# One form of softmax sums for all 24 head pairs, weight buffers released earlier, and two kinds of stores issued by GpSimd

## The chip, the cores and the metric

The kernel runs on one core of a Trainium2 chip (trn2). The metric is the device time in microseconds. A core has TensorE (PE, with its weight loads listed apart as PEld), VectorE (DVE), ScalarE (ACT), GpSimd (POOL) and SyncE (SP), which here issues nearly all transfers of the 16 DMA engines. Each engine takes its instructions in the order in which the program wrote them for it.

## The reference

Three layers run one after the other on 4 sequences of 448 tokens (12 heads of 64, 768 channels):

```python
scores = cap * tanh(q @ k.T / sqrt(64) / cap)
attn = exp(scores - scores.max(-1)); attn /= attn.sum(-1) + 1e-9
x = attn @ v                                   # per head, then 768 channels
...
xk = mu_k*x + (1-mu_k)*x_prev; xr = mu_r*x + (1-mu_r)*x_prev
v = relu(xk @ w_k)**2 @ w_v                    # 768 -> 1024 -> 768
x = sigmoid(xr @ w_r) * v
...
theta = x @ w_theta
y = w_tok_r @ (x*cos(theta)) + w_tok_i @ (x*sin(theta))
u = x + y
out = u + relu(u @ w_ch)
```

The weights come as 64-bit floats, and the kernel turns them into pairs of 16-bit halves (high and low) itself.

## The kernel before, in words

The whole program is a list of operations with engine, planned duration, rank, and the buffers read and written. `Plan.order` (L149) simulates it once on the host with the planned durations and takes, whenever an engine is free, the ready operation of lowest rank; the order that comes out is the program's order on every engine. All transfers stand in the plan as one queue named `DMA`; which engine issues one is decided by the call inside the operation (`nc.sync` is SP, `nc.gpsimd` would be GpSimd). Planned durations therefore move the order of everything, while real waits are semaphores.

**Attention (to about 365 us).** 24 pairs of heads, one after the other, with the products of the first layer of earlier sequences (`kmm`, `rmm`, in `units`, L783 to L785, three matmuls per step: high by high, high by low, low by high) filled in between. Of a pair, `scores` makes the scores (L649, L653), ACT takes tanh and exp, `attend` adds three of the four blocks on DVE (L739), and then one of two forms makes the sums over keys and their reciprocals. `narrow`, for the first 12 pairs (`WIDE = 12`): 16 small matmuls (L676, L680) put the sums of 8 groups of 112 queries on 8 bands of 16 rows, DVE takes a reciprocal of 112 columns (L687), and four matmuls with a 128-column weight (`spread`, L692) spread it over the rows; ACT or DVE brings the product with v out of PSUM (`avo`), and DVE multiplies (L704). `wide`, for the last 12: the fourth block is added first (`fold`, L745, two operations a pair), two matmuls of 448 columns (L712) give the sums on all rows, the reciprocal has 448 columns (L718), and one DVE operation scales the product (L729). Both take the product with v in 10 matmuls. Then come `mxd`, `mxk`, `mxh`, `mxl` (L751 to L758), which mix neighbouring tokens and split into halves.

**Second layer's values (about 417 to 560 us).** `values` (L893): `kd` is loaded again (L900) and split (`k2h`, `k2l`), `vmm` multiplies by w_v (24 matmuls for each of 24 units, two PSUM buffers), a stored gate is loaded into one of five buffers `z` (L906), ACT takes a sigmoid (L907), DVE multiplies (L909), and the store `stx` (L912) writes the result to DRAM. It is loaded again by L941 and L950. The buffer `z` is free when that store has landed.

**Third layer (about 468 us to the end).** `angles`, `mixes`, `channels`: matmuls at L957 to L959, L987 to L989, L1009 to L1011. At the end of a unit DVE adds (L1014), and `sto` (L1015) stores the result.

**Weights.** `group` (L515) and `tokens` (L863) load raw 64-bit weights into one of two buffers `w` (L530, L869), rebuild 32-bit values in one of three buffers `f` (`bits`: a rescaling, L454 to L458, then DVE L461, L464, L467), and take their size: `squares` (L491) squares them on ACT (L495) with an accumulated sum; the squares themselves are of no use, and are written over the raw buffer `w`. PE adds the sums (L500), and three small DVE operations follow. Then come high and low halves (`whi`, `wlo` L543, L885), which go into memory that opens late for w_theta and the token weights (`o_r2`, after the last pair) and for w_ch (`o_l2`, after the last `kmm` and `rmm`). The w_k weights take their size another way (`early`).

Of the kernel before, what the change touches and what calls it, by code (L numbers as in the profile page):

```python
# [7 lines left out]
F32 = mybir.dt.float32  # L8
# [4 lines left out]
AF = mybir.ActivationFunctionType  # L13
ALU = mybir.AluOpType
# [4 lines left out]
B, H, S, D = 4, 12, 448, 64  # L19
# [5 lines left out]
SH = S // 2  # L25
# [5 lines left out]
KT = 7  # L31
# [217 lines left out]
def v1(n):  # L249
    return 0.17 + n / 940.0  # L250
# [6 lines left out]
def act(n):  # L257
    return 0.17 + n / 1150.0
# [19 lines left out]
def body(nc, tc, exact, qk, v, cap, mu_k, mu_r, w_k, w_v, w_r, w_th, w_tr, w_ti, w_ch, out):  # L278
    P = Plan()
    op = P.op  # L280
    ENG = {"ACT": nc.scalar, "DVE": nc.vector, "POOL": nc.gpsimd}
    SLOT = 7.9
    WIDE = 12
    WV0, WV1 = 190.0, 28.0
    WT0, WT1, WO0, WC0, WC1 = 1440.0, 10.0, 1510.0, 1660.0, 20.0
    K20, VM0, VM1 = 390.0, 1500.0, 100.0
# [21 lines left out]
    def tt(n, half=False):  # L308
        return {"POOL": pool(n) - 0.00021 * n * half, "DVE": v1(n)}
# [4 lines left out]
    xd = [[Buf(tile=dr.tile([128, S], F32, name=f"xd{b}_{m}")) for m in range(KD)] for b in range(B)]  # L314
# [55 lines left out]
    def small(n=1):  # L370
        used[0] += n
        return Buf(tile=scal[:, used[0] - n:used[0]])
# [115 lines left out]
        op("PE", 0.3, rank, lambda: nc.tensor.matmul(ps.t[:, 0:1], unit[0:w].to_broadcast([w, 128]), d.t[0:w], start=True, stop=True), r=[d], w=[ps], name="bcast")  # L488
        return ps

    def squares(rank, parts, d):  # L491

        ps = Buf(c_ps)
        for a, (f, val, n, dead) in enumerate(parts):
            op("ACT", act(n) + 0.19, rank, lambda a=a, val=val, n=n, dead=dead: nc.scalar.activation(out=dead.t[:, 0:n], in_=val(), func=AF.Square, accum_out=d.t[:, a:a + 1]),  # L495
               r=[f] if f is not dead else [], w=[dead, (d, a)], name="norm")

        def total():
            for a in range(len(parts)):
                nc.tensor.matmul(ps.t[:, 0:1], unit.to_broadcast([128, 128]), d.t[:, a:a + 1], start=(a == 0), stop=(a == len(parts) - 1))  # L500
        op("PE", 0.2 + 0.1 * len(parts), rank, total, r=[d], w=[ps], name="bcast")
        return ps
# [12 lines left out]
    def group(rank, src, dst, m, inv, nb, after=(), early=False):  # L515

        sw, n = small(), 128 * nb
        vals, parts = [], []
        for a in range(len(dst)):
            w, f = Buf(w_s), Buf(f_s)  # L520
            vals.append(f)

            def half(i, w=w):
                return w.t[:, 0:2 * n].bitcast(U32).rearrange("p (n two) -> p n two", two=2)[:, :, i]

            def val(f=f):
                return f.t[:, 0:n]

            def ld(w=w, a=a):
                nc.sync.dma_start(out=w.t[:, 0:2 * n].bitcast(U32).rearrange("p (i n) -> p i n", i=nb),  # L530
                                  in_=src[n * a:n * a + n, 256 * m:256 * m + 256].rearrange("(i p) n -> p i n", p=128))
            op("DMA", 0.03 + n / 350, rank - 12, ld, w=[w], after=[o_open1], name="wld")
            bits(rank, lambda h=half: h(1), lambda h=half: h(0), val, val, n, w, f, f)
            parts.append((f, val, n, 128 if early else w))
        size(rank, grams(rank, [parts], small()) if early else squares(rank, parts, small(len(parts))), inv, m, sw)
        for a, f in enumerate(vals):
            def part(i, a=a):
                return dst[a].t[:, :, i, 128 * m:128 * m + 128]

            def val(f=f):  # L540
                return f.t[:, 0:n].rearrange("p (i n) -> p i n", i=nb)
            op({**cs(n), "DVE": (v1 if nb % 2 else v2)(n) + 0.06}, 0, rank, lambda e, val=val, part=part: copy(e, part(0), val(), sw.t), r=[f, sw], w=[(dst[a], (m, 0))], after=after, name="whi")
            grouped.append(op("DVE", v1(n) + 0.06, rank, lambda val=val, part=part: nc.vector.scalar_tensor_tensor(  # L543
                out=part(1), in0=val(), scalar=sw.t, in1=part(0), op0=ALU.mult, op1=ALU.subtract),
               r=[f, sw, (dst[a], (m, 0))], w=[(dst[a], (m, 1))], name="wlo"))
# [14 lines left out]
    for b in range(B):  # L560
        R = (2 * NP * b - 7.1) * SLOT if b else 3
        vb = v[NP * b:NP * b + NP].rearrange("g p n -> (g p n)").rearrange("(p n) -> p n", p=128)
        parts = []
        n = 2 * DM
        for c in range(2):
            t = Buf(w_s)
            op("DMA", 0.03 + n / 700, R - 10, lambda t=t, c=c, vb=vb: nc.sync.dma_start(out=t.t, in_=vb[:, c * n:(c + 1) * n]), w=[t], after=[o_open1], name="ldm")
            parts.append([(t, lambda t=t: t.t, n, 128)] if b == 0 else (t, lambda t=t: t.t, n, t))
        size(R, squares(R, parts, small(2)) if b else grams(R, parts, small()), small(), 0, sv[b])
        times(R, sv[b], qi, sx[b])  # L570
        inverse(R, sx[b], ix[b], 0.0, 2.0)
# [14 lines left out]
    last1 = []  # L586
# [79 lines left out]
            op("ACT", act(n * S) + 0.08, A + 3 + 1.8 * c, lambda th=th: nc.scalar.activation(out=th.t, in_=th.t, func=AF.Exp, scale=cap_t),  # L666
               w=[th], name="exp", table="exp")

    def narrow(A, x, sxb, th, vn, z, sp, rs, ps):

        def sums():

# [4 lines left out]
            for k in range(2):  # L677
                for h, i in ((0, 0), (0, 1), (1, 0), (1, 1)):
                    c = 32 * (2 * h + i)
                    nc.tensor.matmul(sp.t[c:c + 32, 0:SQ], ones[:, 1 + i, k], th[3].t[:, h, SQ * k:SQ * k + SQ], start=False, stop=(k == 1))  # L680
        op("PE", 0.74, A, sums, r=[z, th[3]], w=[sp], name="sums")

        def den():

# [5 lines left out]
        def spread():  # L690
            for i in range(4):
                nc.tensor.matmul(sp.t[:, SQ * i:SQ * i + SQ], live["row"][:, i].rearrange("p h d -> p (h d)"), rs.t, start=True, stop=True)  # L692
        op("PE", 0.8, A + 2, spread, r=[rs], w=[sp], name="spread")

        def av():
            for c in range(3):
# [6 lines left out]
        op({"ACT": act(S) + 0.09, "DVE": 0.7}, 0, A + 3, lambda e: copy(e, x.t[:, 1:S + 1], ps.t[:, 0:S], sxb.t), r=[ps, sxb], w=[x], name="avo")  # L703
        last1.append(op("DVE", v1(S), A + 6, lambda: nc.vector.tensor_tensor(out=x.t[:, 1:S + 1], in0=x.t[:, 1:S + 1], in1=sp.t[:, 0:S], op=ALU.mult), r=[sp], w=[x], name="norm"))  # L704

    def wide(A, x, sxb, th, vn, z, sp, ps):

        rs = lambda: x.t[:, 1:S + 1]

        def sums():  # L710
            for h in range(2):
                nc.tensor.matmul(sp.t[64 * h:64 * h + 64, 0:S], unit.to_broadcast([128, D]), z.t[:, h], start=True, stop=True, skip_group_check=True)  # L712
        op("PE", 0.74, A, sums, r=[z], w=[sp], name="sums")

        def den():
            if exact:
                nc.vector.tensor_scalar(out=rs(), in0=sp.t[:, 0:S], scalar1=1e-9, scalar2=None, op0=ALU.add)
            nc.vector.reciprocal(out=rs(), in_=rs() if exact else sp.t[:, 0:S])  # L718
        op("DVE", 2.95, A + 1, den, r=[sp], w=[x], name="den")

        def av():
            for c in range(3):
                for h in range(2):
                    nc.tensor.matmul(ps.t[64 * h:64 * h + 64, 0:S], vn.t[0][:, h, c], th[c].t[:, h], start=(c == 0), stop=False, skip_group_check=True)  # L724
            for i in range(2):
                for h in range(2):
                    nc.tensor.matmul(ps.t[64 * h:64 * h + 64, SH * i:SH * i + SH], vn.t[1][:, i, h], th[3].t[:, h], start=False, stop=True, skip_group_check=True)
        op("PE", 3.02, A + 0.5, av, r=[vn, *th], w=[ps], name="av")
        last1.append(op("DVE", v1(S) + 0.06, A + 4, lambda: nc.vector.scalar_tensor_tensor(  # L729
            out=x.t[:, 1:S + 1], in0=ps.t[:, 0:S], scalar=sxb.t, in1=rs(), op0=ALU.mult, op1=ALU.mult), r=[ps, sxb], w=[x], name="norm"))  # L730

    def attend(g):
        A = g * PAIR + 10
        th, vn = thb[g], vnb[g]
# [4 lines left out]
            op("DVE", v1(2 * S), A - 4 + i, lambda i=i: nc.vector.tensor_tensor(out=z.t, in0=th[0].t if i == 1 else z.t, in1=th[i].t, op=ALU.add),  # L739
               r=[th[0], th[1]] if i == 1 else [th[i]], w=[z], name="sum")  # L740

        if g >= WIDE:
            for i in range(2):
                p, q = slice(64 * i, 64 * i + 64), slice(SH * i, SH * i + SH)
                op(tt(S), 0, A - 1 + 0.5 * i, lambda e, p=p, q=q: e.tensor_tensor(out=z.t[p, :, q], in0=z.t[p, :, q], in1=th[3].t[p], op=ALU.add), r=[th[3]], w=[(z, i)], name="fold")  # L745
            wide(A, x, sx[b], th, vn, z, sp, ps)
        else:
            narrow(A, x, sx[b], th, vn, z, sp, rs, ps)
        R = A + 7
        d, t0 = Buf(mx_s), Buf(mx_s)  # L750
        op(tt(S), 0, R, lambda e: e.tensor_tensor(out=d.t, in0=x.t[:, 1:S + 1], in1=x.t[:, 0:S], op=ALU.subtract), r=[x], w=[d, (t0, "x")], name="mxd")  # L751
# [111 lines left out]
    def tokens(rank):  # L863
        fo = []
        for i in range(KT):
# [9 lines left out]
            def fv(f=f):  # L875
                return f.t
            bits(rank, lambda h=half: h(1), lambda h=half: h(0), fv, fv, S, raw, f, f, [o_r2])
            fo.append((f, fv, S, raw))
        size(rank, squares(rank, fo, small(KT)), io, 0, so)
        tiny(rank, lambda: nc.vector.tensor_scalar(out=iw.t, in0=io.t, scalar1=2.0 ** 49, scalar2=None, op0=ALU.mult), r=[io], w=[iw])  # L880

        tiny(rank, lambda: nc.vector.tensor_scalar(out=tb.t, in0=io.t, scalar1=2.0 ** 70, scalar2=1.0, op0=ALU.mult, op1=ALU.add), r=[io], w=[tb])
# [10 lines left out]
    def values(b):  # L893
# [10 lines left out]
        for m, ps in units("vmm", b, wv, KD, k2, VM0 + VM1 * b, []):  # L904
# [4 lines left out]
            op("DVE", v1(S) + 0.06, 0.0, lambda z=z, ps=ps, b=b, m=m: nc.vector.scalar_tensor_tensor(  # L909
                out=z.t, in0=ps.t[:, 0:S], scalar=vsc[b].t[:, m:m + 1], in1=z.t, op0=ALU.mult, op1=ALU.mult),  # L910
               r=[ps, vsc[b]], w=[z], name="x")
            op("DMA", 0.65, 0.0, lambda z=z, t=xd[b][m]: nc.sync.dma_start(out=t.t, in_=z.t), r=[z], w=[xd[b][m]], name="stx")  # L912
            op("DVE", v1(S), 0.0, lambda z=z, b=b, m=m: nc.vector.tensor_reduce(out=xmx[b].t[:, m:m + 1], in_=z.t, axis=AX.X, op=ALU.max, apply_absolute_value=True),
               r=[z], w=[(xmx[b], m)], name="xmax")
        inverse(0.0, xmx[b], sz[b], 2.0 ** -100, 2.0 ** -13, KD)
# [84 lines left out]
    def channels(b, ms):  # L1000
        for m in ms:
# [10 lines left out]
                op("PE", 0.57, rk, mm, r=[u, (wc[0], (m, 0)), (wc[0], (m, 1))], w=[ps], name="cmm")  # L1012
            op("ACT", act(S) + 0.08, rk, lambda ps=ps, t=t, m=m: nc.scalar.activation(out=t.t, in_=ps.t[:, 0:S], func=AF.Relu, scale=icu[b].t[:, m:m + 1]), r=[ps, icu[b]], w=[t], name="rel")  # L1013
            op(tt(S), 0, rk, lambda e, t=t, x=x: e.tensor_tensor(out=x.t, in0=t.t, in1=x.t, op=ALU.add), r=[t], w=[x], name="res")  # L1014
            fin.append(op("DMA", 0.65, rk, lambda x=x, m=m: nc.sync.dma_start(out=out[m, :, b * S:(b + 1) * S], in_=x.t), r=[x], name="sto"))  # L1015

    for b in range(B):
        gates(b, range(KD), T2 + ST * (6 * b - 9.1) if b else T2 - 45)
# [74 lines left out]
```

## Time and profile before

| | |
|---|---|
| median of 3 runs | 805.9 us (805.28 to 806.34) |
| profiled execution | 805.84 us, of which the profile's span is 804.0 us |
| PE busy | 770.6 us (96%) |
| DVE, ACT, POOL busy | 563.6 us (70%), 440.8 us (55%), 92.6 us (12%) |
| DMA queues | SP's: 116592 packets, 113.86 MB; ACT's: 168 packets, 0.01 MB; GpSimd issues none |

Busy time is a union of the engine's instructions; matmuls overlap each other, so their listed durations (0.35 us) are longer than their spacing (0.19 us). Idle time of an engine that is not the bound costs nothing.

### The profile page before, as it was taken

The numbers are of one execution on the slowest core, as the hardware profiler recorded it, in microseconds if no ns is written. First come the engines' busy times: TensorE is split into PE (matmuls) and PEld (weight loads), VectorE is DVE, ScalarE is ACT, GpSimd is POOL, SyncE is SP. The second block draws the span as 40 slices with busy tenths as digits, with TensorE's granted clock in tenths as the row PEclk, the third lists the DMA queues.
The fourth block names the chain that finished last, engine by engine and source line by source line (L and its number), as shares of the span: only waits on it lengthen the run. The fifth ranks groups of instructions, "written<-read, shape, count | busy, mean of one in ns | idle before, by whom it ended". The sixth has DMA issues, their size and how long they took to land.

```text
span 804.0 us, 12769 instructions
## 1 busy us (share of the span) xinstructions
PE 770.6 (96%) x4924; PEld 386.0 (48%) x4924; DVE 563.6 (70%) x1014; ACT 440.8 (55%) x677; POOL 92.6 (12%) x99
## 2 busy tenths in 40 slices
PE   5989999999999999998999889999999999999996
PEld 2445455454444444443555445555555555555553
DVE  2888897967778899879657768966856544645531
ACT  4889877878775875755526434355635333222201
POOL 1214403201130120101001000101201000000000
PEclk9999999999999999999999999999999999999999
DMA  8855455455343434225556866553535333324402
GB/s 258 257 173 181 158 180 191 138 171 184 113 136 99 139 92 157 97 75 172 176 191 221 296 193 203 185 152 84 123 60 136 82 92 92 90 65 98 99 28 73
DMA packets 116829, 114.76 MB, mean 143 GB/s; under 512 B 55820, under 2 KB 108824, under 8 KB 116760
## 3 DMA queue, kind: packets, MB, share of 16 engines
q1 hardware_dynamic: 116592, 113.86, 46.8%
q8 instruction: 40, 0.66, 0.3%
q14 instruction: 29, 0.24, 0.1%
q10 hardware_dynamic: 168, 0.01, 0.0%
HBM read 78.98 MB, written 23.86 MB: 128 GB/s over the span
## 4 chain that ended last, share of the span: by engine, by line
PE 87%; DMA 5%; DVE 4%; ACT 2%; issue 1%; SPq 1%; ACTq 0%; DVEq 0%
PE one L783 12%; PE one L784 11%; PE one L785 11%; PE big L653 7%; PE q L989 4%; PE q L987 4%; PE q L988 4%; PE one L724 4%; PE one L1010 3%; PE one L1009 3%; PE one L1011 3%; PE one L698 3%; PE q L957 2%; PE q L959 2%; PE q L958 2%; DMA w<-in_v 2%
## 5 line engine op out<-in xcount | busy, mean ns | idle before, releaser
L662 ACT ACTIVATE th<-big,tsc 128x896 f32<-128x896 f32 x72 | 70.1, 1002 | 22.6 <-PE big L653 22.4
L653 PE MATMUL big<-qk 64*64 64x448 f32 x576 | 67.8, 571 | 8.2 <-DMA qk<-in_qk 7.7
L783 PE MATMUL one<-k,wv 128*128 128x448 f16 x192 | 68.3, 356 | 6.2 <-DVE z L909 6.2
L666 ACT ACTIVATE th<-th,cap_t 128x896 f32<-128x896 f32 x72 | 73.0, 1039 | 0.0
L783 PE MATMUL one<-sl,wk 128*128 128x448 f16 x192 | 68.5, 357 | 2.4 <-ACT g L794 1.9
L784 PE MATMUL one<-sl,wk 128*128 128x448 f16 x192 | 68.2, 355 | 0.9 <-POOL sl L758 0.9
L784 PE MATMUL one<-k,wv 128*128 128x448 f16 x192 | 68.2, 355 | 0.0
L785 PE MATMUL one<-k,wv 128*128 128x448 f16 x192 | 68.1, 355 | 0.0
L785 PE MATMUL one<-sl,wk 128*128 128x448 f16 x192 | 68.1, 355 | 0.0
L989 PE MATMUL q<-wo,zt 128*128 128x448 f16 x168 | 59.2, 352 | 0.0
L987 PE MATMUL q<-wo,zt 128*128 128x448 f16 x168 | 59.2, 352 | 0.0
L988 PE MATMUL q<-wo,zt 128*128 128x448 f16 x168 | 59.2, 352 | 0.0
L1013 ACT ACTIVATE z<-one,scal 128x448 f32<-128x448 f32 x24 | 15.1, 627 | 71.9 <-PE one L1011 71.9
L783 PE MATMUL one<-sl,wr 128*128 128x448 f16 x144 | 50.9, 354 | 0.0
L785 PE MATMUL one<-sl,wr 128*128 128x448 f16 x144 | 50.7, 352 | 0.0
L784 PE MATMUL one<-sl,wr 128*128 128x448 f16 x144 | 50.7, 352 | 0.0
L973 DVE SCALAR_TENSOR_TENSOR cs<-xf,scal,cs 128x896 f32<-128x896 f32 x24 | 27.6, 1150 | 31.6 <-DMA xf<-xd 24.2
L718 DVE RECIPROCAL xt<-one 128x448 f32<-128x448 f32 x12 | 35.5, 2956 | 14.0 <-PE one L712 14.0
L758 POOL TENSOR_TENSOR sl<-mx,sl 128x448 f16<-128x448 f32 x24 | 29.5, 1230 | 119.2 <-ACT sl L294 100.6
L454 ACT ACTIVATE w<-w 128x768 f32<-128x768 f32 (+2 forms) x26 | 21.4, 823 | 35.0 <-DMA w<-in_w_ch 17.4
L1014 DVE TENSOR_TENSOR xf<-z,xf 128x448 f32<-128x448 f32 x24 | 15.0, 624 | 34.4 <-ACT z L1013 34.2
L991 DVE SCALAR_TENSOR_TENSOR xf<-q,scal,xf 128x448 f32<-128x448 f32 x24 | 16.4, 683 | 31.8 <-PE q L989 31.6
(191 smaller groups left out, 1739.5 us busy)
## 6 DMA issues: line engine op xcount, KB each, us to landing
qk<-in_qk SPq DMA_DIRECT2D x23, 448.0 KB, 3.8
kd<-g SPq DMA_DIRECT2D x32, 224.0 KB, 2.0
vn<-in_v SPq DMA_DIRECT2D x24, 256.0 KB, 2.7
w<-in_v SPq DMA_DIRECT2D x8, 768.0 KB, 6.2
w<-in_w_k SPq DMA_DIRECT2D x8, 768.0 KB, 5.1
w<-in_w_v SPq DMA_DIRECT2D x12, 512.0 KB, 4.4
zd<-tmp SPq DMA_DIRECT2D x24, 224.0 KB, 2.6
z<-zd SPq DMA_DIRECT2D x24, 224.0 KB, 2.9
```

The costliest lines, as they stand in the source:

```text
L653: nc.tensor.matmul(ps.t[o, h, 0:S], t.t[p, 1, 128 * c + 64 * i:128 * c + 64 * i + 64], t.t[p, 0], start=True, stop=True)
L662: op("ACT", act(n * S) + 0.08, A + 1 + 1.8 * c, lambda src=src, th=th: nc.scalar.activation(out=th.t, in_=src(), func=AF.Tanh, scale=tsc), ...
L666: op("ACT", act(n * S) + 0.08, A + 3 + 1.8 * c, lambda th=th: nc.scalar.activation(out=th.t, in_=th.t, func=AF.Exp, scale=cap_t), w=[th], ...
L718: nc.vector.reciprocal(out=rs(), in_=rs() if exact else sp.t[:, 0:S])
L724: nc.tensor.matmul(ps.t[64 * h:64 * h + 64, 0:S], vn.t[0][:, h, c], th[c].t[:, h], start=(c == 0), stop=False, skip_group_check=True)
L758: op(tt(S, True), 0, R + i, lambda e, t=t, hi=hi, lo=lo: e.tensor_tensor(out=lo.t, in0=t.t, in1=hi.t, op=ALU.subtract), r=[t, hi], w=[lo], ...
L783: nc.tensor.matmul(ps.t[:, 0:S], wh, xh(), start=(kk == 0), stop=False)
L784: nc.tensor.matmul(ps.t[:, 0:S], wh, xl(), start=False, stop=False)
L785: nc.tensor.matmul(ps.t[:, 0:S], wl, xh(), start=False, stop=(kk == len(xs) - 1))
L987: nc.tensor.matmul(o, z.t[:, 0, i], wo[i].t[:, 0], start=(i == 0), stop=False)
L988: nc.tensor.matmul(o, z.t[:, 1, i], wo[i].t[:, 0], start=False, stop=False)
L989: nc.tensor.matmul(o, z.t[:, 0, i], wo[i].t[:, 1], start=False, stop=(i == KT - 1))
```

## The change

The second form of sums goes, and with it `fold`: all 24 pairs take the first (now named `normal`), whose two planned PE durations are lowered (0.74 to 0.36, 0.8 to 0.47), its instructions being the same. `squares` writes its useless output into the tile that will hold the weight's halves, not over the raw buffer; for that it now waits for the memory of that tile to open (`after`). So a raw buffer is free after L467, not after the square. `stx` and `sto` are issued by GpSimd.

```diff
-    WIDE = 12
...
-    def squares(rank, parts, d):
+    def squares(rank, parts, d, after=()):
...
-        for a, (f, val, n, dead) in enumerate(parts):
-            op("ACT", act(n) + 0.19, rank, lambda a=a, val=val, n=n, dead=dead: nc.scalar.activation(out=dead.t[:, 0:n], in_=val(), func=AF.Square, accum_out=d.t[:, a:a + 1]),
-               r=[f] if f is not dead else [], w=[dead, (d, a)], name="norm")
+        for a, (f, val, n, dead, place) in enumerate(parts):
+            op("ACT", act(n) + 0.19, rank, lambda a=a, val=val, place=place: nc.scalar.activation(out=place(), in_=val(), func=AF.Square, accum_out=d.t[:, a:a + 1]),
+               r=[f] if f not in dead else [], w=[*dead, (d, a)], after=after, name="norm")
...
-            parts.append((f, val, n, 128 if early else w))
-        size(rank, grams(rank, [parts], small()) if early else squares(rank, parts, small(len(parts))), inv, m, sw)
+            parts.append((f, val, n, 128) if early else (f, lambda val=val: val().rearrange("p (i t n) -> p i t n", i=nb, t=2), n, [(dst[a], (m, 0)), (dst[a], (m, 1))],
+                                                                     lambda a=a: dst[a].t[:, :, :, 128 * m:128 * m + 128].bitcast(F32)))
+        size(rank, grams(rank, [parts], small()) if early else squares(rank, parts, small(len(parts)), after), inv, m, sw)
...
-        op("PE", 0.74, A, sums, r=[z, th[3]], w=[sp], name="sums")
+        op("PE", 0.36, A, sums, r=[z, th[3]], w=[sp], name="sums")
...
-        op("PE", 0.8, A + 2, spread, r=[rs], w=[sp], name="spread")
+        op("PE", 0.47, A + 2, spread, r=[rs], w=[sp], name="spread")
...
-    def wide(A, x, sxb, th, vn, z, sp, ps):
...
-        if g >= WIDE:
-            for i in range(2):
...
-            wide(A, x, sx[b], th, vn, z, sp, ps)
-        else:
-            narrow(A, x, sx[b], th, vn, z, sp, rs, ps)
+        normal(A, x, sx[b], th, vn, z, sp, rs, ps)
...
-            fo.append((f, fv, S, raw))
-        size(rank, squares(rank, fo, small(KT)), io, 0, so)
+            fo.append((f, lambda f=f: f.t.rearrange("p (t n) -> p t n", t=2), S, [(wo[i], 0), (wo[i], 1)], lambda i=i: wo[i].t.bitcast(F32)))
+        size(rank, squares(rank, fo, small(KT), [o_r2]), io, 0, so)
...
-            op("DMA", 0.65, 0.0, lambda z=z, t=xd[b][m]: nc.sync.dma_start(out=t.t, in_=z.t), r=[z], w=[xd[b][m]], name="stx")
+            op("DMA", 0.65, 0.0, lambda z=z, t=xd[b][m]: nc.gpsimd.dma_start(out=t.t, in_=z.t), r=[z], w=[xd[b][m]], name="stx")
...
-            fin.append(op("DMA", 0.65, rk, lambda x=x, m=m: nc.sync.dma_start(out=out[m, :, b * S:(b + 1) * S], in_=x.t), r=[x], name="sto"))
+            fin.append(op("DMA", 0.65, rk, lambda x=x, m=m: nc.gpsimd.dma_start(out=out[m, :, b * S:(b + 1) * S], in_=x.t), r=[x], name="sto"))
```

## Rows read from the trace of the kernel before

**Rows 1.** Stages: length, busy us (instructions) of PE, PEld, DVE, ACT, POOL; PEclk, DMA, GB/s

```profile
187.00:365.00 178.00, 177.08 (x1148) 77.86 (x1147) 147.34 (x218) 124.02 (x193) 25.66 (x22) 1.00 0.37 118
365.00:385.00 20.00, 16.97 (x81) 8.06 (x80) 18.97 (x27) 11.54 (x23) 2.55 (x2) 0.91 0.53 177
...
440.00:485.00 45.00, 37.41 (x195) 19.24 (x194) 31.55 (x73) 18.56 (x32) 2.86 (x4) 0.97 0.72 243
485.00:780.00 295.00, 295.00 (x1564) 153.41 (x1563) 179.14 (x317) 111.52 (x172) 14.78 (x11) 1.00 0.42 105
780.00:804.00 24.00, 17.99 (x96) 9.10 (x93) 3.91 (x7) 3.80 (x6) 0.00 (x0) 0.98 0.17 61
```

**Rows 2.** Timeline of PE: start, us, instruction; small sums, spread, wide sums, with neighbours

```profile
125.37 0.35 PE L785 MATMUL one<-sl,wk 128*128 128x448 f16 x1
125.65 0.59 PE L676 MATMUL one<-pz,ones 128*32 128x112 f32 x16
...
126.56 0.36 PE L783 MATMUL one<-sl,wk 128*128 128x448 f16 x1
...
128.65 0.35 PE L785 MATMUL one<-sl,wk 128*128 128x448 f16 x1
128.84 1.04 PE L692 MATMUL one<-rs,row 128*128 128x112 f32 x8
129.72 0.35 PE L783 MATMUL one<-sl,wk 128*128 128x448 f16 x1
129.91 0.35 PE L784 MATMUL one<-sl,wk 128*128 128x448 f16 x1
...
223.22 0.35 PE L785 MATMUL one<-sl,wk 128*128 128x448 f16 x1
223.50 0.97 PE L712 MATMUL one<-pz,unit 128*64 128x448 f32 x4
224.40 0.36 PE L783 MATMUL one<-sl,wk 128*128 128x448 f16 x1
```

**Rows 3.** Groups by line, whole span: instruction, count, busy us, mean ns, idle before

```profile
L718 DVE RECIPROCAL xt<-one 128x448 f32<-128x448 f32 x12 | 35.5, 2956 | 14.0 <-PE one L712 14.0
...
L495 ACT ACTIVATE w<-f 128x768 f32<-128x768 f32 (+1 forms) x30 | 22.5, 751 | 11.9 <-issue 6.6 <-DVE f L467 3.9 <-DVE scal L511 1.4
...
L745 DVE TENSOR_TENSOR pz<-pz,tl 64x448 f32<-64x448 f32 x20 | 14.1, 706 | 0.5
...
L687 DVE RECIPROCAL rs<-one 128x112 f32<-128x112 f32 x12 | 10.2, 852 | 2.9 <-PE one L680 2.7
```

**Rows 4.** Timeline of PE where it waited: in brackets idle before, and its end

```profile
369.66 0.35 PE L783 MATMUL one<-sl,wk 128*128 128x448 f16 x1 [0.38 <-ACT sl L294]
370.88 0.35 PE L784 MATMUL one<-sl,wk 128*128 128x448 f16 x1 [0.87 <-POOL sl L758]
...
373.61 0.53 PE L783 MATMUL one<-sl,wk 128*128 128x448 f16 x1 [1.62 <-ACT g L794]
...
482.80 0.55 PE L783 MATMUL one<-k,wv 128*128 128x448 f16 x1 [2.85 <-DVE z L909]
```

**Rows 5.** Waits of SP's own queue: who for whom, total us, times, longest

```profile
SPq L530 <- ACT w L495: 43.9, 23, 4.4
...
SPq L906 <- DMA xd<-z: 26.6, 12, 4.7
...
SPq L912 <- DVE z L909: 20.6, 13, 6.4
```

**Rows 6.** Waits of the other engines, same columns

```profile
POOL xs L291 <- DMA xg<-xd: 19.3, 3, 17.9
...
ACT w L454 <- DMA w<-in_w_ch: 17.4, 6, 5.7
```

**Rows 7.** Transfers by line: issuer, count, KB each, median us from issue to landing

```profile
xd<-z SPq DMA_DIRECT2D x24, 224.0 KB, 3.5
...
out<-xf SPq DMA_DIRECT2D x24, 224.0 KB, 1.9
...
cap_t<-in_cap ACTq DMA_DIRECT2D x1, 0.5 KB, 3.1
```

More of the change, by code (lines that the diff above doesn't have):

```diff
@@ L567, in body @@
             op("DMA", 0.03 + n / 700, R - 10, lambda t=t, c=c, vb=vb: nc.sync.dma_start(out=t.t, in_=vb[:, c * n:(c + 1) * n]), w=[t], after=[o_open1], name="ldm")
-            parts.append([(t, lambda t=t: t.t, n, 128)] if b == 0 else (t, lambda t=t: t.t, n, t))
+            parts.append([(t, lambda t=t: t.t, n, 128)] if b == 0 else (t, lambda t=t: t.t, n, [t], lambda t=t: t.t))
         size(R, squares(R, parts, small(2)) if b else grams(R, parts, small()), small(), 0, sv[b])
@@ L667, in scores, with normal @@
                w=[th], name="exp", table="exp")
-    def narrow(A, x, sxb, th, vn, z, sp, rs, ps):
+    def normal(A, x, sxb, th, vn, z, sp, rs, ps):
         def sums():
@@ L704, in narrow @@
         last1.append(op("DVE", v1(S), A + 6, lambda: nc.vector.tensor_tensor(out=x.t[:, 1:S + 1], in0=x.t[:, 1:S + 1], in1=sp.t[:, 0:S], op=ALU.mult), r=[sp], w=[x], name="norm"))
-    def wide(A, x, sxb, th, vn, z, sp, ps):
[L708 to L724, printed above, removed]
-            for i in range(2):
[L726 to L730, printed above, removed]
     def attend(g):
@@ L740, in attend @@
                r=[th[0], th[1]] if i == 1 else [th[i]], w=[z], name="sum")
-        if g >= WIDE:
-            for i in range(2):
-                p, q = slice(64 * i, 64 * i + 64), slice(SH * i, SH * i + SH)
-                op(tt(S), 0, A - 1 + 0.5 * i, lambda e, p=p, q=q: e.tensor_tensor(out=z.t[p, :, q], in0=z.t[p, :, q], in1=th[3].t[p], op=ALU.add), r=[th[3]], w=[(z, i)], name="fold")
-            wide(A, x, sx[b], th, vn, z, sp, ps)
-        else:
-            narrow(A, x, sx[b], th, vn, z, sp, rs, ps)
+        normal(A, x, sx[b], th, vn, z, sp, rs, ps)
         R = A + 7
```

## The prediction, made before the changed kernel had run

> **What bounds the kernel now.** I read the page first: PE is busy 96% of the span and leads the chain that ended last, so the question for each part of the change is what it does to PE's work, and what to the few stretches in which PE waits. The table of stages shows where those are [rows 1]. From 187 to 365 us, where the last 12 pairs run, PE is busy for 177.08 of 178 us: it waits 0.92 us in all, and whatever PE gets there in addition is paid in full. From 485 to 780 us it never waits. Between them lie two soft places. From 365 to 385 us PE idles 3.03 us and its mean granted clock is 0.91 (part of the stretch at 1.2 GHz rather than 2.4, after the waits), which costs about 20 x 0.09 = 1.8 us more. From 440 to 485 us it idles 7.59 us, and a clock of 0.97 costs 45 x 0.03 = 1.35 us. So 4.8 and 8.9 us could be had back at most, 13.7 together; what is idle from 780 us on is the end of the program. Then I read the timeline of PE around the small instructions that change [rows 2] and around the waits [rows 4], the waits of SP's queue and of the engines [rows 5, 6], and the transfers [rows 7].
>
> **Part 1: the sums.** What counts is how much later the next 16-bit matmul starts, since the listed durations overlap. Matmuls of the first layer follow each other every 0.19 us (129.91 - 129.72). Around the small sums the spacing is 126.56 - 125.37 = 1.19 us, so they insert 1.00 us; around `spread` it is 129.72 - 128.65 = 1.07, so that inserts 0.88; around the wide sums it is 224.40 - 223.22 = 1.18, so these insert 0.99 [rows 2]. The first form costs PE 1.88 us a pair and the second 0.99. Twelve pairs change from the second to the first: 12 x (1.00 + 0.88 - 0.99) = **+10.7 us of PE time**, nearly all of it `spread`. The planned durations of 0.36 and 0.47 do not make it shorter; the same instructions are issued. Other neighbours change the insertion a little: the 8 instructions of `spread` span 1.04 us themselves, and with a switch on either side I bound the term by 10.0 and 14.6 (12 x 1.22). I take 10.7, read from isolated cases.
>
> On DVE the part takes away 12 reciprocals of 2.956 us for 12 of 0.852, a gain of 25.3 us, and 20 folds of 0.706, 14.1 us [rows 3] (the other four folds are GpSimd's); it gives back 12 evacuations `avo` on ACT or DVE. That is some 38 us less of DVE's work, and I cost it at nothing from 187 to 365 us: DVE is busy for 147 of 178 us there and PE waited 0.92 us for all others together [rows 1]. It counts in one place, after the last pair, where nothing is left to fill in. There the path from sums to the scaled product loses a reciprocal of 2.96 us and gains one of 0.85 and a `spread` of 0.88, so it is about 1.2 us shorter. That is the size of the first two waits behind this pair, 0.38 and 0.87 us together [rows 4]. The third, 1.62 us for `kev` on ACT (L794), which stands behind splits of `k2` there, need not go. With a part of the clock's 1.8 us I take **-2.0** for 365 to 385 us, between 0 and -4.8.
>
> **Part 2: the squares.** Removed is a wait of the raw buffers: SP's queue stood 43.9 us in 23 waits at L530 for the square that frees the buffer [rows 5]. Now L467 frees it, earlier by the square itself and by its wait for ACT, and since two buffers take turns the gain adds up from load to load. The instructions stay as they are: 30 squares of 0.751 us and the 7 of the tokens [rows 3]. If ACT is slower at the scattered output, it is off the path. What is late in 440 to 485 us is the preparation of w_ch: ACT waits 17.4 us in 6 waits for its raw loads [rows 6], up to 5.7 us each, with splits and sigmoids queued behind it; DVE's multiplication L909 then comes late, PSUM's two buffers stay full, and PE waits (2.85 us in the longest case) [rows 4]. Loads that start earlier take some of this away. Added is a wait: the squares of w_theta, three of which can be ready early, cannot run before the last pair is done. PE's small additions L500 and the halves wait for them; the third layer uses the weights from about 468 us on, 100 us later, and that covers it. Without that cover, see rival D.
>
> **Part 3: the stores.** `stx` moves from SP to GpSimd. SP no longer stands at L912 (20.6 us in 13 waits) with loads queued behind it [rows 5]. It still stands at L906, 26.6 us, until a store has landed and its `z` is free; that part stays. The trace has no transfer issued by GpSimd. The nearest rows are the stores themselves on SP, 3.5 us in the median, and 1.9 us for the results, and the one transfer on another queue, 3.1 us on ACT's [rows 7]. A gain is not excluded, since a store would no longer queue behind a 768 KB load on SP. I put parts 2 and 3 together at **-4.9** for 440 to 485 us, a little over half of the 8.9 us, between 0 and -8.9, and split it as SP's waits 43.9 and 20.6 stand to each other: -3.3 and -1.6. From 485 us on PE never waits [rows 1], so `sto` and the loads behind it cost nothing until the last store, which nothing hides. If it takes as long as now, 0; if as long as the median `stx`, 1.6 us; I take **+0.8**, in the middle.
>
> SP's row shows queueing: 20.6 us in which it stood at L912 with other loads to issue [rows 5]. The Trainium skill, in "DMA: Bandwidth & Descriptors", the section that says issuing engines are not separate queues, holds that a second issuing engine saves only the time it takes to start a transfer, as all run on the same 16 engines. By that rule the 1.6 us would not come, since SP is not short of issue time, and the sum would be 812.0 in place of 810.4; by the row some comes, because what SP loses is time at a wait. Rival E is that case.
>
> **The sum.** 805.84 (profiled execution, of which 804.0 is the span; 0.06 below the median) + 10.7 - 2.0 - 4.9 + 0.8 = **810.4 us**, slower by 0.6%.
>
> **The rivals.**
> - **B, faster or even: the soft places go wholly.** With all 13.7 us back, 805.84 + 10.7 - 13.7 + 0.8 = 803.6. For it: the raw loads are what ACT waits for, and the release comes earlier in a chain of many loads. Against it: the loads still depend on the plan's guess of their landing, the `z` cycle of loads and stores stays, and 1.62 us at 373.61 hang on the order of ACT. It decides when over 13.0 of the 13.7 us come back (12.3 if part 1 costs its lower bound), and from 9.8 on the change is even. The plan's new order might also shorten waits before 90 us, which I did not count.
> - **C, slower still: stores stuck on GpSimd.** GpSimd's compute instructions wait in order, and one waited 17.9 us for a load [rows 6]. A store behind such a one lands that much later. Five `z` buffers at 24 x 0.19 = 4.6 us a unit cover 23 us, and a turn of load, sigmoid, product and store (two landings of 3.5 us, and the work between) takes an estimated 10; so a store 17.9 us late would stop PE for about 5 us. Time: 810.4 + 5 = 815.4. It decides where one store is over 13 us late. Against it: GpSimd has only 4 compute instructions in that stage [rows 1].
> - **D, slower still: the squares' new wait hurts.** Three squares of 0.75 + 0.19 us land on ACT after the last pair, in front of `kev`, where PE already waited for it [rows 4]: up to +2.8, and none of the 2.0 back: 810.4 + 4.8 = 815.
> - **E, the moved stores give nothing**: nothing that PE needed stood behind L912 on SP. The 1.6 us fall away: 812.0. Against it: w_ch's raw loads are on that queue [rows 6]. By the skill's rule above it would be so.
>
> **How the numbers follow.** Forecast's case, cost in full and part of the waits back: 0.45, with its own range 806.5 to 814 (of it 0.07 within 0.2%). E: 0.15. B: 0.20 (0.13 faster, 0.07 even). C: 0.10. D: 0.10. A measurement here tells 0.2%, or 1.6 us, from no change: faster means below 804.3, slower above 807.5. That makes faster 0.13, same 0.14, slower 0.73. The range runs from B at 803.6 to just above C and D, 817: below it B with a cheaper first part, above it several mishaps or the dear end of part 1, together under 0.2.
>
> **What would show it.** In the profile after: 24 groups of L692 with 0.88 us between their neighbours, none of L712; the end of the last pair about 10 us later; PE's idle time from there to the third layer down from 10.6 us to about 5; SP's waits for L495 gone and those for L909 moved to GpSimd; the last store's landing later by under 2 us. The prediction is wrong if `spread` inserts less than read, if PE's waits go altogether, or if new ones open where none were, because the plan, whose PE durations are lowered by 0.7 us a pair, puts the work in another order.

## The result

The changed kernel takes 812.92 us in the median (812.05 to 815.25) against 805.82 us; the ratio is 1.0089, interval 1.0069 to 1.0110: slower by 7.1 us. Run again on another chip, beside runs of parts of the change, it took 816.66 us, a ratio of 1.0128 (1.0105 to 1.0150), or 10.3 us slower. Every ratio below is against the kernel before on the same chip. The profiled execution took 813.48 us, of which 811.6 us are the span.

The profile after, busy times of its page:

```profile
PE 781.0 (96%) x5356; PEld 402.6 (50%) x5356; DVE 538.3 (66%) x1022; ACT 433.7 (53%) x660; POOL 112.4 (14%) x144
```

PE's busy time grows from 770.6 to 781.0 us, by 10.4; the span grows by 7.6; so PE idles 2.8 us less in all. DVE loses 25.3 us (some 38 were forecast).

The table of stages after, columns as in [rows 1]; the last pair now ends near 378 us, so most stages are cut later, by up to 25 us:

```profile
190.00:382.00 192.00, 192.00 (x1561) 96.68 (x1558) 125.30 (x231) 121.49 (x189) 15.35 (x16) 1.00 0.37 122
382.00:410.00 28.00, 25.21 (x136) 13.59 (x135) 24.83 (x55) 15.58 (x31) 1.98 (x2) 1.00 0.64 200
410.00:440.00 30.00, 29.81 (x164) 16.17 (x163) 20.52 (x40) 14.77 (x31) 1.29 (x2) 1.00 0.81 260
440.00:500.00 60.00, 56.95 (x309) 30.42 (x308) 50.27 (x132) 30.47 (x48) 11.06 (x17) 1.00 0.73 240
500.00:785.00 285.00, 285.00 (x1510) 147.82 (x1509) 164.04 (x272) 105.18 (x161) 26.90 (x38) 1.00 0.40 98
```

While the last pairs run PE now waits for nothing (192.00 of 192). The place after the last pair still costs 2.8 us of idle time, and the second soft place has come down from 7.59 us [rows 1] to 3.05. PEclk is 1.00 in every stage shown, against 0.91 and 0.97 in the two soft places before; that was the fortune of this execution, as the last section shows.

PE's timeline after, around a `spread` and at the longest wait (columns as in [rows 2, 4]):

```profile
228.22 0.35 PE L753 MATMUL one<-sl,wk 128*128 128x448 f16 x1
228.41 1.04 PE L692 MATMUL one<-rs,row 128*128 128x112 f32 x8
229.29 0.35 PE L751 MATMUL one<-sl,wk 128*128 128x448 f16 x1
...
391.95 0.35 PE L751 MATMUL one<-sl,wk 128*128 128x448 f16 x1 [2.55 <-ACT g L762]
```

`spread` inserts 229.29 - 228.22 - 0.19 = 0.88 us here, as in [rows 2], and it stands in all 24 pairs. The two short waits behind the last pair in [rows 4] are gone; the third, for `kev` on ACT, grew from 1.62 to 2.55 us.

Of the groups by line (columns as in [rows 3]) those that changed:

```profile
L692 PE MATMUL one<-rs,row 128*128 128x112 f32 x192 | 26.2, 280 | 1.0 <-DVE rs L687 1.0
...
L687 DVE RECIPROCAL rs<-one 128x112 f32<-128x112 f32 x24 | 20.5, 856 | 18.8 <-PE one L680 18.6
...
L494 ACT ACTIVATE wt<-f 128x768 f32<-128x768 f32 x6 | 5.0, 838 | 1.6 <-DVE scal L510 1.1 <-DMA tmp<-kd 0.4
```

The 35.5 us of long reciprocals and the folds [rows 3] are replaced by 12 more short ones (20.5 us for 24); a square writes into the half's tile `wt` and takes 0.84 us.

Waits after, of SP's queue and of GpSimd (columns as in [rows 5, 6]):

```profile
SPq L874 <- DMA xd<-z: 46.4, 12, 8.6
SPq L529 <- DVE f L466: 40.6, 18, 5.9
...
POOL xd L880 <- DVE z L877: 128.8, 15, 53.8
```

SP no longer stands for the squares or for DVE's product; it stands for L466 (the old L467), the loads' new releaser, and in total hardly less than it stood for the squares (40.6 us in 18 waits, 43.9 in 23 before [rows 5]). It stands longer than before for a store to land (46.4 us, 26.6 before [rows 5]). GpSimd waits for the product instead.

The transfers that moved (columns as in [rows 7]):

```profile
xd<-z POOLq DMA_DIRECT2D x24, 224.0 KB, 2.5
...
out<-xf POOLq DMA_DIRECT2D x24, 224.0 KB, 2.2
```

The second layer's stores land 2.5 us after issue in the median, 1.0 less than on SP; those of the results 0.3 more [rows 7].

The end of the program has a cost that no step or rival of the prediction named. The instructions of the closing line of the launch, number and duration in ns (least, median, most), first the changed kernel's:

```profile
L1057 POOLq DRAIN  x3: 40/100/4056, 806.8 to 811.3; - x3
```

then the kernel before's:

```profile
L1089 POOLq DRAIN  x3: 34/76/122, 618.3 to 803.6; - x3
```

GpSimd's drain, 0.12 us at 618 us before, takes 4.06 us and begins at 806.8 us, after the last store has landed (806.6 us); the program waits for it. From DVE's last addition to the end of the span it is 811.6 - 803.8 = 7.8 us in place of 804.0 - 799.3 = 4.7.

### The profile page after: what moved, and what is told of

Same layout as the page of the kernel before. It is cut to its first block, busy times and chain, and to the rows that moved or that the text cites. A ratio compares the mean times of both kernels' runs of the same rounds, so it can differ in the third digit from the quotient of the medians.

```text
span 811.6 us, 13643 instructions
## 1 busy us (share of the span) xinstructions
PE 781.0 (96%) x5356; PEld 402.6 (50%) x5356; DVE 538.3 (66%) x1022; ACT 433.7 (53%) x660; POOL 112.4 (14%) x144
## 4 chain that ended last, share of the span: by engine, by line
PE 62%; issue 23%; DVE 6%; DMA 5%; ACT 2%; POOL 2%; ACTq 0%; POOLq 0%; SPq 0%; DVEq 0%
PE one L751 11%; PE one L752 10%; PE one L753 10%; PE big L653 6%; PE one L698 6%; PE one L692 3%; PE one L701 2%; POOL out L983 1%; PE one L676 1%; PE q L925 1%; PE q L927 1%; PE q L926 1%; PE q L957 1%; PE q L956 1%; PE q L955 1%
## 5 line engine op out<-in xcount | busy, mean ns | idle before, releaser
L698 PE MATMUL one<-th,vn 128*64 128x448 f32 x288 | 59.4, 548 | 0.0
L726 POOL TENSOR_TENSOR sl<-mx,sl 128x448 f16<-128x448 f32 x26 | 31.5, 1213 | 147.4 <-ACT sl L293 117.0
L983 POOL DMA_DIRECT2D out<-xf x24 | 13.1, 544 | 202.1 <-DVE xf L982 202.1
L979 PE MATMUL one<-w_u,wc 128*128 128x448 f16 x108 | 38.1, 352 | 0.0
```

The costliest lines, as they stand in the source:

```text
L726: op(tt(S, True), 0, R + i, lambda e, t=t, hi=hi, lo=lo: e.tensor_tensor(out=lo.t, in0=t.t, in1=hi.t, op=ALU.subtract), r=[t, hi], w=[lo], ...
L979: nc.tensor.matmul(ps.t[:, 0:S], wl, u.t[:, 0], start=False, stop=(kk == KD - 1))
```

## The experiments

**All stores back on SP.** In this and the other cuts of stores, ... stands for the rest of the line.

```diff
-... nc.gpsimd.dma_start(out=t.t, in_=z.t), r=[z], w=[xd[b][m]], name="stx")
+... nc.sync.dma_start(out=t.t, in_=z.t), r=[z], w=[xd[b][m]], name="stx")
...
-... nc.gpsimd.dma_start(out=out[m, :, b * S:(b + 1) * S], in_=x.t), r=[x], name="sto"))
+... nc.sync.dma_start(out=out[m, :, b * S:(b + 1) * S], in_=x.t), r=[x], name="sto"))
```

> The changed kernel with both kinds of stores back on SP; the order of PE, ACT and DVE is the changed kernel's. Theory T (the moved stores cost at the end of the program, through GpSimd's drain of 4.06 us there and a slower last landing, and give little before): the stretch from DVE's last addition to the end falls from 7.7 us to about 4.7, PE's waits between 440 and 500 us stay near 3 us, total about 810 (3 us below the changed kernel's 813). Theory P (as the prediction had it: the moved stores give 1.6 us between 440 and 500 us and cost 0.8 at the end): about 813.5 to 814.

1.0115 (1.0081 to 1.0149), 814.15 us: between the changed kernel's two ratios. In the profile the end is 4.4 us after DVE's last addition, 3.4 less than in the changed kernel's, yet the spans are equal (811.6): PE comes to its end 3.4 us later, and 1.9 of that are lost near 393 us, where the granted clock is 0.94 in the stage from 382 to 410 us and the changed kernel's execution had 1.00. Theory T is shown for the end; for the total the spread of the times is wider than what was looked for. Theory T fits the second soft place too: PE idles 60 - 56.51 = 3.49 us from 440 to 500 us. The second layer's matmuls in the changed kernel's order, with their first and last start in us, the stores on GpSimd in both executions of the changed kernel, then on SP in this run:

```profile
L751 PE MATMUL one<-k,wv x192: 349/352/363, 427.6 to 551.3; 128*128 128x448 f16 x192
L751 PE MATMUL one<-k,wv x192: 349/352/581, 433.2 to 558.9; 128*128 128x448 f16 x192
...
L751 PE MATMUL one<-k,wv x192: 349/352/363, 430.5 to 554.7; 128*128 128x448 f16 x192
```

They take 123.7 and 125.7 us with the stores on GpSimd (125.3 in the next run, where `stx` stays there too) and 124.2 on SP, so in this order no gain from moving `stx` can be told.

**The results alone back on SP.**

```diff
-... nc.gpsimd.dma_start(out=out[m, :, b * S:(b + 1) * S], in_=x.t), r=[x], name="sto"))
+... nc.sync.dma_start(out=out[m, :, b * S:(b + 1) * S], in_=x.t), r=[x], name="sto"))
```

> The changed kernel with only the stores of the results back on SP; the second layer's stores stay on GpSimd. Theory T1 (the long drain at the end belongs to a store that GpSimd issued shortly before): POOL's drain falls below 0.5 us, total about 810. Theory T2 (any transfer issued by GpSimd makes the drain at the end long, however early it was): the drain stays near 4 us, the stretch from DVE's last addition to the end stays at 7 us or more, total about 812.5.

1.0108 (1.0069 to 1.0147), 814.62 us. Its drain:

```profile
L1057 POOLq DRAIN  x3: 40/96/2114, 629.1 to 814.5; - x3
```

Neither theory had it: the drain takes 2.11 us, half of 4.06, but at 629 us, where GpSimd has come to the end of its own program and nobody waits. The end of the program is 5.0 us after DVE's last addition. The totals looked for, 810 and 812.5, were both lower than what was measured.

**The stores alone**, in the kernel before; PE, ACT and DVE have its order.

```diff
-... nc.sync.dma_start(out=t.t, in_=z.t), r=[z], w=[xd[b][m]], name="stx")
+... nc.gpsimd.dma_start(out=t.t, in_=z.t), r=[z], w=[xd[b][m]], name="stx")
...
-... nc.sync.dma_start(out=out[m, :, b * S:(b + 1) * S], in_=x.t), r=[x], name="sto"))
+... nc.gpsimd.dma_start(out=out[m, :, b * S:(b + 1) * S], in_=x.t), r=[x], name="sto"))
```

> The kernel before with both kinds of stores issued by GpSimd, and nothing else; PE, ACT and DVE have the order of the kernel before. Theory T: the end is 3.0 us longer, the stretch from 440 to 485 us about as before (PE idle 7.6 us): about 808.9. Theory P: 440 to 485 us gives 1.6 back: about 807.3. A store stuck behind GpSimd's compute instructions (rival C of the prediction) would add a new wait of PE of up to 5 us: 813.

1.0021 (1.0001 to 1.0041), or +1.7 us. Its stage from 440 to 490 us, its drain, and its PE wait there:

```profile
440.00:490.00 50.00, 44.61 (x230) 22.93 (x229) 37.44 (x90) 22.38 (x38) 9.51 (x13) 0.97 0.79 249
...
L1089 POOLq DRAIN  x3: 40/100/4055, 800.9 to 805.4; - x3
...
PE one L783 <- DVE z L909: 4.2, 2, 2.3
```

Both theories hold in part. PE idles 5.39 us there where the kernel before idles 7.59 us. That alone proves little: in the next two runs, which leave all but one of these stores, or all of them, on SP, it idles 5.31 and 5.94 us in this stage, at a clock of 0.93. The second layer's matmuls tell it better, since PE has the same order in all four: the kernel before, this run, then the next two runs.

```profile
L783 PE MATMUL one<-k,wv x192: 349/352/581, 416.6 to 547.3; 128*128 128x448 f16 x192
L783 PE MATMUL one<-k,wv x192: 349/352/581, 416.5 to 545.6; 128*128 128x448 f16 x192
L783 PE MATMUL one<-k,wv x192: 349/352/581, 418.5 to 548.7; 128*128 128x448 f16 x192
L783 PE MATMUL one<-k,wv x192: 349/352/581, 415.4 to 546.2; 128*128 128x448 f16 x192
```

From first to last start they take 129.1 us with the stores moved, and 130.7, 130.2 and 130.8 without, so in this order moving `stx` gives 1.1 to 1.7 us, near the 1.6 of the prediction. The end is 3.45 us longer. The difference, 1.8 to 2.4 us, is near the time measured.

**One store alone on GpSimd**, in the kernel before.

```diff
-... lambda z=z, t=xd[b][m]: nc.sync.dma_start(out=t.t, in_=z.t), r=[z], w=[xd[b][m]], name="stx")
+... lambda z=z, t=xd[b][m], e=(nc.gpsimd if b == m == 0 else nc.sync): e.dma_start(out=t.t, in_=z.t), r=[z], w=[xd[b][m]], name="stx")
```

> The kernel before with one single transfer, the first store of the second layer's values at about 425 us, issued by GpSimd. Theory T1: the drain at the end is as short as in the kernel before (0.08 us), total 805.8. Theory T2: the drain is near 4 us though the transfer ended 370 us earlier, total about 808.5.

1.0017 (1.0000 to 1.0034), 806.74 us.

```profile
L1089 POOLq DRAIN  x3: 40/88/217, 620.1 to 804.9; - x3
```

The drain takes 0.22 us, not 4, and at 620 us: T2 falls. The 1.1 us by which the median lies higher are not the drain's; the interval reaches 1.

**The last six results on GpSimd**, in the kernel before.

```diff
-... lambda x=x, m=m: nc.sync.dma_start(out=out[m, :, b * S:(b + 1) * S], in_=x.t), r=[x], name="sto"))
+... lambda x=x, m=m, e=(nc.gpsimd if b == B - 1 else nc.sync): e.dma_start(out=out[m, :, b * S:(b + 1) * S], in_=x.t), r=[x], name="sto"))
```

> The kernel before with only the last six stores of results issued by GpSimd, so that GpSimd issues six transfers in all, the last at the very end. If the drain at the end is proportional to the number of transfers that GpSimd issued (0.22 us with 1, 2.11 with 24, 4.06 with 48), it takes about 0.6 us, and the program about 0.8 us more than the kernel before. If it takes long whenever a transfer of GpSimd has just ended, it takes about 4 us, and the program 3 us more.

1.0006 (0.9988 to 1.0023), level.

```profile
L1089 POOLq DRAIN  x3: 40/100/626, 801.2 to 802.4; - x3
```

The drain is 0.63 us, at the very end, right after a store: its length goes with the number of transfers that GpSimd issued. 0.12, 0.22, 0.63, 2.11 and 4.06 us for 0, 1, 6, 24 and 48 are a line of 0.08 us a transfer.

**The squares alone**, in the kernel before: the changed `squares`, `group` and `tokens`, as in the diff ahead of the prediction.

```diff
-            parts.append((f, val, n, 128 if early else w))
+            parts.append((f, val, n, 128) if early else (f, lambda val=val: val().rearrange("p (i t n) -> p i t n", i=nb, t=2), n, [(dst[a], (m, 0)), (dst[a], (m, 1))],
+                                                                     lambda a=a: dst[a].t[:, :, :, 128 * m:128 * m + 128].bitcast(F32)))
```

> The kernel before with the squares' new place and nothing else (two forms of sums, stores on SP). Theory of the prediction: raw loads of w_ch start earlier, and PE's idle time between 440 and 485 us, 7.6 us in the kernel before, falls by half or more: 802 to 803.5. Rival D (the squares of w_theta, which now wait for the last pair, hold ACT and PE up after it): PE's waits from 365 to 385 us grow from 3.0 to about 6 us: 807 to 808.

1.0074 (1.0044 to 1.0103), 811.19 us: slower by 6 us. Two of its stages:

```profile
187.00:365.00 178.00, 174.96 (x1117) 75.56 (x1115) 143.35 (x214) 116.23 (x177) 22.97 (x21) 1.00 0.36 116
...
440.00:490.00 50.00, 46.34 (x241) 24.33 (x240) 39.77 (x90) 21.26 (x33) 7.65 (x8) 0.97 0.81 258
```

From 440 to 490 us PE idles 3.66 us, half of before, as the theory said. But from 187 to 365 us, where it idled 0.92 us [rows 1], it idles 3.04: the plan, given other releases, put a fold of DVE too late for the sums of a pair (one wait of 1.9 us). In the whole execution PE still idles 2.1 us less than before (805.9 - 774.6 = 31.3 us against 33.4); its span is 1.9 us longer because its busy time grew by 4.0 us (774.6 against 770.6) with the same instructions in another order, and what lengthened them was not traced. The profiled execution (807.73 us) was nearly the fastest of the seven, so the trace accounts for 1.9 us of the difference and not for the rest; where the slower ones lose it is open.

**The sums alone**, in the kernel before, all 24 pairs in the first form, with the planned durations as they were and with the lowered ones.

```diff
-    WIDE = 12
+    WIDE = 24
```

> The kernel before with the small sums for all 24 pairs and nothing else, planned PE durations as they were (0.74 and 0.8). Theory of the prediction: PE gets 10.7 to 11.5 us more work, paid in full where PE never waits, and the waits after the last pair lose about 2: 814 to 815.5. Rival (38 us less work on DVE let PE's later waits go as well, without the other parts): 807 to 809.

> As the run with the sums alone, but with the lowered planned durations of the changed kernel (0.36 and 0.47), which move only the order. If the planned durations matter for the time, it differs from the run with the sums alone by more than 2 us; if not, both are at 814 to 815.5.

1.0174 (1.0154 to 1.0195) and 1.0115 (1.0091 to 1.0140): +14.0 and +9.3 us with the same instructions. Two stages of the first:

```profile
410.00:440.00 30.00, 27.66 (x151) 15.09 (x152) 13.91 (x34) 9.19 (x20) 0.00 (x0) 1.00 0.64 201
440.00:500.00 60.00, 52.04 (x264) 26.19 (x264) 44.90 (x100) 26.84 (x44) 4.89 (x6) 0.96 0.73 222
```

and of the second:

```profile
410.00:440.00 30.00, 29.40 (x159) 15.63 (x158) 18.64 (x46) 11.30 (x23) 0.60 (x1) 1.00 0.58 190
440.00:500.00 60.00, 54.38 (x291) 28.79 (x290) 43.94 (x97) 28.54 (x49) 5.83 (x8) 0.98 0.76 252
```

The order with the old durations has 10.3 us of idle time in these 90 us, the other 6.2: the planned durations move where PE waits. The rival, that the relief of DVE alone lets the later waits go, is out.

**The changed kernel beside its parts.**

> The changed kernel itself, on the same chip as the parts. If the parts add up, its distance from the kernel before is that of the sums alone (lowered planned durations) plus that of the squares alone plus the 1.3 us measured for the stores alone: about 10 - 3 + 1.3 = 8 us, so 813 to 814. If the parts act on the same waits (squares and sums both shorten waits that exist once), the sum of the parts is several us below the whole.

1.0128 against 1.0115 for the sums alone with the same durations: 1 us more, with the stores' 1.7 in it. So the squares give about 0.7 us in this company, with intervals of 2 us on either side, that is, nothing that can be told. PE's busy time in this execution is 789.9 us, 8.9 more than in the first one. The sum of the parts measured alone, 1.0115 + 0.0074 + 0.0021, is 1.021, more than the whole: parts do not add, and in the opposite way to the one named.

**Part 1 undone in the changed kernel**, results on SP.

```diff
+    WIDE = 12
...
-        normal(A, x, sx[b], th, vn, z, sp, rs, ps)
+        if g >= WIDE:
...
+            wide(A, x, sx[b], th, vn, z, sp, ps)
+        else:
+            normal(A, x, sx[b], th, vn, z, sp, rs, ps)
```

> The changed kernel with the two forms of sums restored (the second for the last 12 pairs) and the stores of the results on SP; the squares' place, the lowered planned durations and the second layer's stores on GpSimd stay. Against the run with only the results on SP (1.0108 of the kernel before) this undoes part 1 alone. If part 1 is the 11.5 us of PE work that the account of the changed kernel shows, paid in full, this is at 803 to 804 us, a little faster than the kernel before. If the squares or the new order cost something of their own, as the run with the squares alone suggests (1.0074), it stays at 807 or more.

1.0091 (1.0058 to 1.0124), 813.31 us: against 1.0108 with the first form everywhere. Taking away some 11 us of PE work gives back 1.4 us, or nothing that the intervals can tell (the two ratios come from different chips). Two of its stages:

```profile
190.00:372.00 182.00, 178.12 (x1131) 77.47 (x1129) 149.53 (x225) 118.72 (x182) 24.58 (x25) 0.99 0.39 124
...
400.00:440.00 40.00, 37.00 (x203) 20.06 (x202) 24.80 (x54) 18.23 (x38) 0.00 (x0) 1.00 0.67 208
```

PE waits 3.9 us while the last pairs run and 3.0 us from 400 to 440 us, where the changed kernel waits 0 and 0.2 us (from 410 us). In the whole of the two profiles PE idles 813.8 - 780.1 = 33.7 us here and 814.7 - 785.3 = 29.4 with the first form everywhere; and the granted clock here is 0.96 from 50 to 90 us, 0.99 from 190 to 372 and 0.97 from 440 to 500, where that run has 1.00, which by these means costs another 1.6 + 1.8 + 1.8 us. So in these two executions much of the work taken away came back as waits and as lower clock.

**Other orders and borders**, in the kernel before: the lowered durations alone, and the second form for 15 pairs in place of 12.

```diff
-        op("PE", 0.74, A, sums, r=[z, th[3]], w=[sp], name="sums")
+        op("PE", 0.36, A, sums, r=[z, th[3]], w=[sp], name="sums")
...
-        op("PE", 0.8, A + 2, spread, r=[rs], w=[sp], name="spread")
+        op("PE", 0.47, A + 2, spread, r=[rs], w=[sp], name="spread")
```

> The kernel before with the planned PE durations of the first form lowered (0.36 and 0.47) and nothing else: the same instructions in another order. If the lower durations are what took about 4 us off the run with the sums alone, the time falls here too, by some 2 us for half the pairs; if that was the luck of one order, it is level with the kernel before or on either side of it.

```diff
-    WIDE = 12
+    WIDE = 9
```

> The kernel before with the second form of sums for the last 15 pairs in place of 12. If PE pays 0.9 us a pair for the first form also between 130 and 190 us, and VectorE (84% busy there) can carry three more long reciprocals, the time falls by 2.5 us, to 0.997 of the kernel before. If VectorE becomes the bound there, new waits of PE take the gain away, and it is level or slower.

1.0060 (1.0033 to 1.0087) and 1.0051 (1.0032 to 1.0069). The first has the same instructions as the kernel before and is 4.8 us slower by its order alone. In the second, PE's stages from 90 to 365 us are nearly full (99.59 of 100, 173.59 of 175), and then:

```profile
375.45 0.53 PE L783 MATMUL one<-sl,wk 128*128 128x448 f16 x1 [6.13 <-ACT sl L294]
```

VectorE, 23.1 us busy of the 25 from 365 to 390 us, is behind with the last pair, and PE pays 6.13 us at one place, more than twice the 2.7 us of work that three pairs save (3 x 0.89). No version that ran beats the kernel before.

## Why the prediction was right, and where it was not

**Sign and size.** 810.4 was forecast, 812.9 measured, within the range, slower as forecast. Of the miss of 2.5 us the larger part is one term, the end of the program. The rest of the agreement is partly luck. From profile to profile the span grows by 7.6 us: 3.1 at the end, -7.9 in the two soft places (4.8 of idle time and 3.15 of clock, against 6.9 forecast), and 12.4 elsewhere, of which part 1 is 11.6 by the count below. The clock's share was a draw of that execution; on the second chip the same kernel was slower by 10.3 us, more than twice the forecast's 4.6, and only just inside the range. The parts measured one by one do not add up to either time.

**Part 1, +10.7.** The term was read nearly rightly: 0.88 us for an isolated `spread` after as before. Counted in both traces from each instruction's start to the next one's, waits left out, the 24 spreads take 22.9 us against 11.6 for 12, the small sums 21.8 against 10.9, and the wide sums took 10.6: 11.6 us more, inside the bounds of 10.0 and 14.6. That PE's busy time grows by 10.4 is no check of the term: the busy time before holds some 3 us of lower clock from the soft places, and in the second execution of the changed kernel it is 19.3 us longer than before. With the lowered durations the sums alone cost 9.3 us (7.3 to 11.3), where 10.7 - 2.0 = 8.7 stood in the prediction, but with the old ones 14.0, and the lowered durations alone cost 4.8; so this agreement, too, is that of one order. The step "I cost it at nothing" for the 38 us of DVE's work is where it was not right in general. It holds for the order of the kernel before, in which PE waits 0.92 us in that stretch. In the changed order the second form would have made PE wait 3.9 us there and 3.0 later, as part 1 undone shows, and the work of the first form fills time that would have been idle. Relative to the kernel before, part 1 adds about the work that was said; relative to the changed kernel without it, it costs next to nothing.

**After the last pair, -2.0.** The mechanism is as told: the two short waits of together 1.25 us are gone and the third stays. But the third grew to 2.55 us, behind splits of `k2` that wait for their loads on ACT, so idle time fell only from 3.03 to 2.8 us. In that execution the clock's 1.8 us came back too, which makes the 2.0, but not in three others of this order of PE (0.94 there, with 2.33 to 3.35 us of idle time). In those the place gives between +0.2 and -0.8 us, so the term was over 1 us too large.

**Part 2, -3.3.** The wait at L530 left and the idle time it was to shorten did fall, with the squares alone from 7.59 to 3.66 us. Of these 3.9 us, 2.1 went to new waits in a stretch that had hardly any, and PE's busy time grew by 4.0. Alone the part costs 6 us; in the changed kernel it gives about 0.7, not told from nothing. The step that failed is that earlier loads change nothing but their own waits; they also change the plan's order on every engine. Rival D named another place (squares in front of `kev`); there the waits are 3.4 us with the squares alone, 3.07 before, so that is not where it went.

**Part 3, -1.6 and +0.8.** The first is borne out in the order of the kernel before (1.1 to 1.7 us in the second layer's matmuls). In the changed order it is not shown: with the stores on SP these matmuls take no longer than with them on GpSimd, and rival E, that the moved stores give nothing, is not ruled out there. The Trainium skill's rule behind rival E ("DMA: Bandwidth & Descriptors", section "Issuing engines are not separate DMA queues": a second issuing engine saves only the time of starting transfers) would have had no gain in either order; the traces agree with it in the changed one (124.2 us on SP; 123.7, 125.7 and 125.3 on GpSimd) and not in the order before (129.1 against 130.2 to 130.8). Rival C did not come about: in the changed kernel no store was issued more than 0.8 us after DVE's product. The second term is the one mis-sized: the last landing comes 0.3 us later, as bounded, but behind it stands GpSimd's drain, and the end is 3.1 us longer, not 0.8.

**B** needed 13 of the 13.7 us of the two soft places back; 7.9 came in the profiled execution, 3.15 of them from the clock.

## What to carry to other kernels

Where an order is planned by a list scheduler from guessed durations, an edit is two edits: its work and a new order. Here all seven other orders were slower, one with no change of instructions at all by 4.8 us; measure a part in the order in which it will stand, and read the waits of a stage before calling relief there worthless. Idle time moves from run to run; where two kernels have the same order, compare the time between the same two instructions. An engine's work that is free while PE is full is no longer free where the next edit makes PE wait for that engine. Before a transfer is moved to GpSimd as the last thing of a program, look at what GpSimd does at its end.

## What the runs showed of the hardware that was not expected

GpSimd's drain at the end of its program grows by 0.08 us for each transfer it has issued: 0.12, 0.22, 0.63, 2.11 and 4.06 us for 0, 1, 6, 24 and 48. All of these transfers are alike (224 KB), so whether their number or their size counts is not told apart. It is free when GpSimd is done early (at 620 to 629 us) and in the way when it issues the last store.

Two executions of the same changed kernel, on two chips, differ by 7.8 us in span, and what differs is mostly the granted clock (PE's busy time differs by 8.9 us with the same instructions in the same order). Three stages of the slower one (span 819.4 us):

```profile
50.00:90.00 40.00, 39.61 (x402) 19.51 (x394) 32.01 (x57) 33.12 (x44) 16.34 (x13) 0.93 0.49 150
...
382.00:410.00 28.00, 25.67 (x132) 13.39 (x130) 23.83 (x47) 16.30 (x34) 4.21 (x4) 0.94 0.60 179
...
440.00:500.00 60.00, 56.62 (x302) 30.33 (x301) 47.84 (x111) 33.54 (x53) 11.83 (x18) 0.97 0.74 243
```

In the faster one all of these are at 1.00, with about the same idle time (2.79 and 3.05 us in the last two, 2.33 and 3.38 here). A wait of 2.55 us was followed by full clock in one execution, one of 2.13 us at the same place by a mean of 0.94 in the other, which costs 28 x 0.06 = 1.7 us. So one profile of a kernel with such waits shows one draw. The changed kernel's was lucky in its clock, though not in its time: 813.48 us lies above its median of 812.92.
